# First transfers in another order, and two weight passes pinned on VectorE, in a windowed attention and three-way maxout kernel

## The chip, the cores and the metric

The kernel runs on one core of one Trainium2 chip. The metric is the device time of one execution in microseconds (us). All values are float32, or float32r, the same 32 bits read by TensorE as a matmul operand.

## What is computed

The reference, cut to what matters:

```python
# q, k, v: (8, 8, 576, 64): batch B, heads H, sequence S, head size D
scores = scale * np.matmul(q, k.transpose(0, 1, 3, 2))
bias = slopes[:, None, None] * (-np.abs(rel))[None, :, :]      # rel = i - j
mask = (rel >= 0) & (rel < 128)                                # a causal window of 128
scores = np.where(mask, scores + bias[None], -1e9)
attn = np.exp(scores - np.max(scores, axis=-1, keepdims=True))
attn = attn / (np.sum(attn, axis=-1, keepdims=True) + 1e-9)
o = np.matmul(attn, v)
x = o.transpose(0, 2, 1, 3).reshape(B * S, H * D)              # (4608, 512)
h = np.maximum(np.maximum(x @ w1, x @ w2), x @ w3)             # w1..w3: (512, 768)
return h @ w_out                                               # w_out: (768, 512)
```

## The kernel before, in words

**Attention.** The 64 heads are taken in pairs of a batch; a pair is a task (32 tasks, four to a batch). A task has rows in blocks of 128, the last block of 64 shared by two neighbouring tasks, so two tasks make nine steps and a batch of eight heads makes 18 (`steps`, `n_steps`). A step's work: `products` (the score matmuls into the PSUM tiles `ps_s` or `ps_m`, line 381, for two steps at once), `score` (on VectorE the copy under a mask, lines 396 and 399, then per head one pass that adds the bias, keeps the row maximum and writes the tile `s`, line 410), `exps` (two exponentials on ScalarE, line 422), `sums_of` (for two steps: ScalarE adds the epsilon to the sums, line 428, VectorE takes the reciprocal, line 429), `normalise` (GpSimd, line 436, or ScalarE, line 441), `turn` (four transposes on TensorE into `pt`, line 450, copied out by ScalarE and spread by GpSimd) and `mix` (the matmuls with v into `ps_x`, lines 495 and 517).

**Weights.** The 12 weight groups (`w_all`; 0 to 8 are w1 to w3 in slices, 9 to 11 are w_out) are each 1 MB. `fetch(g)` starts the transfer of a group into one of two raw buffers (tag `hs2`, shown as `hs`) on SyncE's queue, line 145. A group is copied as bytes without its first three, so that its words stand shifted; VectorE passes over the bytes and words then form the float32 values. `preparing()` takes the groups in the order 0, 1, 9, 10, 11, 2, ..., 8, each in six parts: `exponents` (for the first four groups, `few`, a clip of the exponent bytes on VectorE, line 156), `convert` (two VectorE passes of 1024 elements: the one that ends at line 165 is called the reduce here, the one at line 172 the shift), and four `part`s. Each part splits 512 columns into a high half on ScalarE (line 196) and a low half on VectorE (line 197), and for parts 2 and 3 TensorE first forms sums of weight blocks (the fold, line 201; line 187 for a low half that is formed there), which need the matrices `plus` (the identity) and `minus`. The results are the tiles `ring` (groups 0 to 8, two groups at a time) and `ow` (9 to 11). Groups 0 to 8 are also stored to HBM (`keep`, line 192) and come back from there for the later batches.

**Maxout.** With the seven-product scheme for 2x2 blocks, each batch has 77 units (`unit`, line 709) of up to 12 matmuls on `xs` (the attention output in high and low halves, `factors_x`) or `hs` (the hidden values, `factors_h`), and their results are combined on ScalarE and VectorE (lines 725, 662, 663).

**Order.** All calls are put in a list of events with a time in steps (`at(when, what, ...)`), sorted, and traced in that order. The scheduler behind the tracing then sets each engine's list by its own estimates of readiness; `tc.keep_in_program_order(x)` holds an instruction behind everything traced before it on its engine. `weights(n)` advances the preparation by n parts' worth: it is called at each step s + 0.2 from step 5 on with 1.6, which makes one or two parts. `spin` puts matmuls without use on TensorE. What stands ahead of the events is traced by hand, at the end of the function: the first transfers, the biases (`slopes`, `slopes_t`, from the tile `dist`), and `plus` and `minus` from `dist[:, 2]`, where the identity is loaded.

Of the kernel before, what the change touches and what calls it, by code (L numbers as in the profile page):

```python
# [15 lines left out]
ALU = mybir.AluOpType  # L16
# [18 lines left out]
def attention_maxout_kernel(  # L35
# [11 lines left out]
    nc = tc.nc  # L47
# [40 lines left out]
    for a in range(2):  # L88
        for d in (slice(0, P),) if a == 0 else (slice(0, D), slice(D, P)):
            nc.gpsimd.affine_select(  # L90
                out=prev[d, a], in_=prev[d, a], pattern=[[1, P]], compare_op=ALU.is_gt, fill=0.0,
# [7 lines left out]
    dist = hs_p.tile([P, 3, P], F32, name="hs")  # L99
# [5 lines left out]
    def slopes_t(pair):  # L105
        for h in range(2):
            d = slice(h * D, (h + 1) * D)
            for j in range(2):
                nc.gpsimd.tensor_scalar(
                    out=bias_t[d, pair, j], in0=dist[d, 1], scalar1=slope(4 * pair + 2 * h + j), scalar2=None,  # L110
                    op0=ALU.mult,
                )

    def slopes(hp):
        for h in (2 * hp, 2 * hp + 1):
            nc.scalar.activation(bias[:, h, :], dist[:, 0], AF.Copy, scale=slope(h))
        nc.gpsimd.affine_select(  # L117
            out=bias0[:, 2 * hp:2 * hp + 2], in_=bias[:, 2 * hp:2 * hp + 2], pattern=[[0, 2], [-1, P]],
            compare_op=ALU.is_ge, fill=-NEG, base=0, channel_multiplier=1,
        )  # L120
# [22 lines left out]
    def fetch(g):  # L143
        r = raws[g] = hs_p.tile([P, 4 * DM + DM // 2], I32, name="hs2", bufs=2)
        nc.sync.dma_start(r.bitcast(U8)[:, :16 * DM - 3], w_all[g].bitcast(U8)[:, 3:])

    def pieces(g):
        r = raws[g]
        x = r[:, :4 * DM].rearrange("p (n w) -> p n w", w=2)
        sign = r.bitcast(I8)[:, :16 * DM].rearrange("p (n b) -> p n b", b=8)[:, :, 4]  # L150
        return x[:, :, 0], x[:, :, 1], sign, r[:, 4 * DM:].bitcast(I8)

    def exponents(g, few):
        _, t, top, small = pieces(g)
        if few:
            nc.vector.tensor_scalar(out=small, in0=top, scalar1=-56.0, scalar2=56.0, op0=ALU.max, op1=ALU.min)
        else:
            nc.scalar.activation(small, top, AF.Relu, bias=-56.0)
            nc.scalar.activation(t.bitcast(F32), top, AF.Relu, scale=-2.0 ** 27, bias=-56.0 * 2.0 ** 27)
# [110 lines left out]
    def preparing():  # L270
        for n, g in enumerate(g_order):
            exponents(g, n < FEW)
            yield
            convert(g, n < FEW)
            yield
            for k in range(4):
                while g < 9 and not ahead(g, k > 0):
                    yield True
                part(g, k)
                if k == 1 and n + 2 < NG:  # L280
                    fetch(g_order[n + 2])
                yield
# [57 lines left out]
    def load(t):  # L340
        b, hp = tasks[t]
        qkt[t] = qk_p.tile([P, 2, S], F32, name="qk")
        for cs in (slice(0, 2 * P), slice(2 * P, S)) if t == 0 else (slice(0, S),):
            nc.sync.dma_start(qkt[t][:, :, cs], qk[b, hp, :, :, cs])

    def load_v(t):
        b, hp = tasks[t]
        vt[t] = v_p.tile([P, NB + 1, P], F32, name="v")
        nc.sync.dma_start(vt[t], v[b, hp])
# [384 lines left out]
    def at(when, what, *args):  # L734
        events.append((when, len(events), what, args))
# [40 lines left out]
            when += pace if u < 77 * b + 63 else O_PACE  # L776
    for u in range(77 * B, 77 * B + 3):
        at(when, unit, u)
    for s in range(5, n_steps + 2):
        at(s + 0.2, weights, 1.6)  # L780
        at(s + 0.7, rest)
    for s in range(1, n_steps, 2):
        at(s + 0.45, spin, SPIN)
# [5 lines left out]
    at(2 * n_steps + LAG_X + shift[2], fix)  # L789
    spin(FIRST_SPIN)  # L790
    load(0)
    load_v(0)
    nc.sync.dma_start(dist[:, 2], c_ident)
    slopes(0)
    slopes_t(0)
    fetch(0)
    nc.scalar.copy(out=plus, in_=dist[:, 2])
    nc.scalar.activation(minus, dist[:, 2], AF.Copy, scale=-1.0)
    load(1)
    fetch(1)  # L800
    for _, _, what, args in sorted(events, key=lambda e: e[:2]):
        what(*args)
# [38 lines left out]
```

## Time and profile before

| | |
|---|---|
| three timed runs | 773.58 us median (770.88, 773.58, 775.7) |
| the profiled execution | 771.28 us, of it 769.5 us span |
| TensorE busy (matmul) | 750.6 us |
| TensorE weight loads | 680.9 us |
| VectorE | 546.0 us |
| ScalarE | 519.0 us |
| GpSimd | 193.5 us |
| transfers | 184.95 MB, mean 240 GB/s |

The span runs from the first instruction to the last; the device time is 1.8 us longer. In rows of the profile PE is TensorE, PEld its weight loads, DVE VectorE, ACT ScalarE, POOL GpSimd and SP SyncE, whose queue starts most transfers. A row of the timeline gives the start, the duration, the engine, the line of the kernel, the operation, what it writes and reads, how many are merged, and in brackets how long the engine had been idle and what ended it.

### The profile page before, as it was taken

Reading aid. Unit: us, or ns where it says so; the run is one execution under the profiler, and the core shown is the slowest. Engines: PE = TensorE matmul, PEld = TensorE weight load, DVE = VectorE, ACT = ScalarE, POOL = GpSimd, SP = SyncE. Lnnn points to the kernel's source line nnn. Section 1 sums busy time; section 2 is a strip of 40 time slices with the busy share of each in tenths; the row PEclk is TensorE's granted clock in tenths of the full one; section 3 lists DMA queues with packets and bytes.
Section 4 is the critical chain, followed back from the end, with each engine's and each line's share of the span. In section 5 each row is a group of like instructions: output and inputs, shape, how many; then the busy total and the mean of one; then the engine's idle time right before and its main releaser. Section 6 shows DMA issues by size and latency. Waiting matters only on the chain.

```text
span 769.5 us, 19396 instructions
## 1 busy us (share of the span) xinstructions
PE 750.6 (98%) x7252; PEld 680.9 (88%) x7257; DVE 546.0 (71%) x1698; ACT 519.0 (67%) x1680; POOL 193.5 (25%) x403
## 2 busy tenths in 40 slices
PE   7898999999999999999999999999999999999998
PEld 3466778889999999999999999999999999999998
DVE  4869788885767847795677847695777847693673
ACT  5798798876678766776676756676676766552342
POOL 4440222311232122221222122221222122343100
PEclk9999999999999999999999999999999999999999
DMA  6772777584898559983888569883898568789721
GB/s 246 246 288 94 271 258 290 219 291 124 282 306 278 191 187 314 306 279 102 293 297 284 182 197 317 292 274 117 284 302 275 185 205 287 263 264 359 232 71 63
DMA packets 43838, 184.95 MB, mean 240 GB/s; under 512 B 4832, under 2 KB 14304, under 8 KB 34912
## 3 DMA queue, kind: packets, MB, share of 16 engines
q0 software_dynamic: 20304, 115.61, 45.5%
q1 hardware_dynamic: 23296, 67.97, 25.2%
q8 instruction: 57, 0.93, 0.5%
q14 instruction: 37, 0.30, 0.1%
q10 hardware_dynamic: 144, 0.13, 0.1%
HBM read 157.74 MB, written 25.95 MB: 239 GB/s over the span
## 4 chain that ended last, share of the span: by engine, by line
PE 67%; DVE 13%; ACT 7%; issue 1%; DVEq 0%; ACTq 0%
PE ps_m L709 54%; PE ps_s L381 4%; PE ps_x L517 4%; PE pt L450 3%; DVE hs L565 3%; DVE t L662 2%; DVE hq L663 2%; ACT p L422 2%; DVE t L568 1%; DVE xs L565 1%; PE pt L201 1%; ACT p L441 1%; ACT t L725 1%; DVE xk L551 1%; ACT hs L564 1%
## 5 line engine op out<-in xcount | busy, mean ns | idle before, releaser
L709 PE MATMUL ps_m<-xs,ring 128*128 128x288 f32 x2916 | 415.7, 297 | 3.1 <-ACT t L725 1.8
L709 PEld LDWEIGHTS ps_m<-xs,ring 128*128 128x128 f32 x2916 | 393.4, 188 | 10.3 <-ACT t L725 6.4
L725 ACT COPY t<-ps_m 128x288 f32<-128x288 f32 x262 | 102.5, 393 | 78.4 <-PE ps_m L709 76.0
L709 PE MATMUL ps_m<-hs,ow 128*128 128x288 f32 x1008 | 141.6, 297 | 1.1 <-DVE hs L565 0.4
L709 PEld LDWEIGHTS ps_m<-hs,ow 128*128 128x128 f32 x1008 | 134.8, 188 | 4.5 <-ACT t L725 1.9
L422 ACT ACTIVATE p<-s,st 128x128 f32<-128x128 f32 x288 | 115.0, 402 | 13.0 <-DVE st L410 12.0
L470 POOL TENSOR_SCALAR_AFFINE_SELECT pp<-pr 128x256 f32<-128x256 f32 x112 | 51.2, 457 | 287.9 <-ACT pr L454 167.2
L317 POOL DMA_DIRECT2D ring<-keep x121 | 65.0, 538 | 203.4 <-PE ps_m L709 196.5
L441 ACT ACTIVATE p<-p,st 128x128 f32<-128x128 f32 x252 | 85.8, 395 | 26.8 <-DVE st L429 26.8
L662 DVE TENSOR_TENSOR t<-ps_m,t 128x288 f32<-128x288 f32 x144 | 64.9, 452 | 50.3 <-PE ps_m L709 34.9
L410 DVE CUSTOM_DVE_ANT_0 s<-ps_s,bias 128x128 f32<-128x128 f32 x240 | 60.8, 285 | 10.5 <-POOL bias L117 4.5
L663 DVE TENSOR_TENSOR hq<-t,hq 128x288 f32<-128x288 f32 x144 | 65.7, 462 | 2.5
L381 PE MATMUL ps_s<-qk 64*64 64x192 f32 (+1 forms) x1088 | 63.3, 317 | 0.8 <-DMA qk<-in_qk 0.4
L517 PE MATMUL ps_x<-pp,v 64*64 64x64 f32 (+3 forms) x1456 | 56.2, 274 | 0.0
L422 ACT ACTIVATION_READ_ACCUMULATOR p<-s,st 128x1 f32 x288 | 55.6, 193 | 0.0
L564 ACT CAST hs<-hq 128x288 fp32r<-128x288 f32 x96 | 40.1, 433 | 22.7 <-DVE hq L663 19.3
L551 DVE TENSOR_TENSOR xk<-ps_x,xk 128x256 f32<-128x256 f32 (+3 forms) x56 | 25.4, 453 | 39.0 <-ACT xk L550 39.0
L517 PEld LDWEIGHTS ps_x<-pp,v 64*64 64x64 f32 x1456 | 42.8, 133 | 11.1 <-issue 9.8
L474 POOL TENSOR_SCALAR_AFFINE_SELECT pp<-pr 128x256 f32<-128x256 f32 (+1 forms) x112 | 50.1, 447 | 1.1
L450 PE MATMUL pt<-plus,p 128*128 128x128 f32 x288 | 48.3, 287 | 1.7 <-POOL p L436 1.0
L450 PEld LDWEIGHTS pt<-plus,p 128*128 128x128 f32 x288 | 30.3, 140 | 20.5 <-issue 14.0
L399 DVE COPY_PREDICATED ps_s<-prev,ps_s 128x256 f32<-128x256 uint8 x105 | 44.3, 422 | 3.7 <-PE ps_s L381 2.3
(123 smaller groups left out, 823.8 us busy)
## 6 DMA issues: line engine op xcount, KB each, us to landing
ring<-keep POOLq DMA_DIRECT2D x60, 1024.0 KB, 7.5
ring<-keep POOLq DMA_DIRECT2D x61, 768.0 KB, 5.9
qk<-in_qk SPq DMA_DIRECT2D x31, 576.0 KB, 5.6
hs<-in_w_all SPq DMA_DIRECT2D x12, 1023.6 KB, 5.6
v<-in_v SPq DMA_DIRECT2D x32, 320.0 KB, 5.6
keep<-ring SPq DMA_DIRECT2D x9, 1024.0 KB, 5.3
outT<-t SPq DMA_DIRECT2D x64, 144.0 KB, 1.8
keep<-ring SPq DMA_DIRECT2D x9, 768.0 KB, 4.9
```

The costliest lines, as they stand in the source:

```text
L317: nc.gpsimd.dma_start(wts[n, a], keep[n % 9][a])
L381: pe(nc.tensor.matmul(ps[j][d:d + D, o:o + k1 - k0], lhsT=qkt[u][j * D:(j + 1) * D, 0, q0:q0 + D], rhs=qkt[u][j * D:(j + 1) * D, 1, k0:k1] ...
L410: nc.vector.tensor_tensor_reduce(out=x, in0=ps[j][:, P:2 * P], in1=below, scale=-0.125, scalar=3.0e38, op0=ALU.add, op1=ALU.min, accum_out ...
L422: nc.scalar.activation(p[:, j], x, AF.Exp, bias=st[:, 0, a, j:j + 1], scale=-1.0, accum_out=st[:, 1, a, j:j + 1])
L441: nc.scalar.activation(p[:, j], p[:, j], AF.Copy, scale=st[:, 2, a, j:j + 1])
L450: pe(nc.tensor.transpose(out=pt[:, a, j], in_=p[:, j], identity=ident))
L470: nc.gpsimd.affine_select(out=old, in_=src, pattern=[[-x, n] for x, n in pat], compare_op=ALU.is_gt, fill=0.0, base=0, channel_multiplier=1,)
L517: pe(nc.tensor.matmul(x[j * D:(j + 1) * D, r, o:o + rhs.shape[1]], lhsT=vv[k, i, j * D:(j + 1) * D], rhs=rhs[k], start=start, stop=True, s ...
L662: nc.vector.tensor_tensor(out=s, in0=ps, in1=e, op=ALU.add)
L663: nc.vector.tensor_tensor(out=h, in0=s, in1=h, op=ALU.max)
L709: pe(nc.tensor.matmul(part_of[n, {2: 0, 5: 0, 6: 0, 3: 1}.get(kk, kk)], lhsT=lt, rhs=rt, start=first, stop=i == len(pairs) - 1, skip_group ...
L725: nc.scalar.copy(out=e, in_=ps)
```

## The change

The calls at the end of the function come in another order. SyncE's first transfers were: q and k of task 0 (in two pieces), v of task 0, the identity, weight group 0, q and k of task 1, weight group 1. Now they are: q and k of task 0, weight group 0, q and k of task 1, v of task 0, weight group 1; and the identity is loaded from ScalarE's queue. The clip of the exponent bytes is held in program order on VectorE for groups 0 and 1, and the first call of `weights` is now an event of its own, at 2.06, with one part; the call at step 5.2 has 0.6 in place of 1.6.

```diff
     def exponents(g, few):
         _, t, top, small = pieces(g)
         if few:
-            nc.vector.tensor_scalar(out=small, in0=top, scalar1=-56.0, scalar2=56.0, op0=ALU.max, op1=ALU.min)
+            x = nc.vector.tensor_scalar(out=small, in0=top, scalar1=-56.0, scalar2=56.0, op0=ALU.max, op1=ALU.min)
+            if g < 2:
+                tc.keep_in_program_order(x)
...
+    at(2.06, weights, 1)
     for s in range(5, n_steps + 2):
-        at(s + 0.2, weights, 1.6)
+        at(s + 0.2, weights, 1.6 if s > 5 else 0.6)
         at(s + 0.7, rest)
...
     load(0)
-    load_v(0)
-    nc.sync.dma_start(dist[:, 2], c_ident)
+    nc.scalar.dma_start(dist[:, 2], c_ident)
+    fetch(0)
     slopes(0)
     slopes_t(0)
-    fetch(0)
+    load(1)
+    load_v(0)
     nc.scalar.copy(out=plus, in_=dist[:, 2])
     nc.scalar.activation(minus, dist[:, 2], AF.Copy, scale=-1.0)
-    load(1)
     fetch(1)
```

With it, lines from 157 to 778 of the kernel move down by two, and those behind by three or more (410 becomes 412, 197 becomes 199, 793 becomes 795).

SyncE's list from its first transfer on, before (`qk`: q and k, `hs_164` and `hs_170`: the raw weights of groups 0 and 1):

```order
L344 DMA qk<-in_qk 128x2x256
L344 DMA qk<-in_qk 128x2x320
L349 DMA v<-in_v 128x640
L793 DMA hs<-in_ident 128x128
L145 DMA hs_164<-in_w_all 128x8189
L344 DMA qk<-in_qk 128x1152
L145 DMA hs_170<-in_w_all 128x8189
```

and of the change:

```order
L346 DMA qk<-in_qk 128x2x256
L346 DMA qk<-in_qk 128x2x320
L145 DMA hs_153<-in_w_all 128x8189
L346 DMA qk<-in_qk 128x1152
L351 DMA v<-in_v 128x640
L145 DMA hs_170<-in_w_all 128x8189
```

The identity has left this list, and v stands three transfers later. In ScalarE's list the identity's transfer stands second, and the casts to `plus` and `minus` stand behind two of the eight biases instead of all eight.

VectorE's list behind the low half of group 0's first fold (`hs_170`: group 1; `ps_m_453` and `ps_m_454`: the scores of steps 10 and 11), before:

```order
L197 TENSOR_TENSOR ring<-ps_m_401,ring 128x2x256
L410 ISA s,st<-ps_s,bias_115 128x128
L410 ISA st 128x1
L165 ISA hs_170<-hs_170 128x1024
L172 SCALAR_TENSOR_TENSOR hs_170<-hs_170 128x1024
L396 COPY_PREDICATED ps_m_453<-prev,ps_m_453 128x128
L429 RECIPROCAL st<-st 128x4
L396 COPY_PREDICATED ps_m_454<-prev,ps_m_454 128x128
```

and of the change, in which the clip (L156) of group 1 stood eight rows ahead before:

```order
L199 TENSOR_TENSOR ring<-ps_m_401,ring 128x2x256
L431 RECIPROCAL st<-st 128x4
L156 TENSOR_SCALAR hs_170<-hs_170 128x1024
L398 COPY_PREDICATED ps_m_453<-prev,ps_m_453 128x128
L398 COPY_PREDICATED ps_m_454<-prev,ps_m_454 128x128
L412 ISA s,st<-ps_m_453,bias 128x128
L412 ISA st 128x1
L412 ISA s,st<-ps_m_454,bias 128x128
L412 ISA st 128x1
L167 ISA hs_170<-hs_170 128x1024
L398 COPY_PREDICATED ps_m_453<-prev,ps_m_453 128x128
L174 SCALAR_TENSOR_TENSOR hs_170<-hs_170 128x1024
```

The reciprocal (of steps 8 and 9) has come ahead of group 1's three passes, and the passes now stand among the masks and scores of steps 10 and 11. Group 0's clip has moved back by one score.

TensorE's list where the fold of group 1 (`ps_m_507`) begins (`ps_m_610` and `ps_m_611`: the scores of steps 14 and 15), before:

```order
L201 MATMUL ps_m_507<-ring,plus 128x256 x2
L495 MATMUL ps_x<-pp,v 64x256 x4
L381 MATMUL ps_s<-qk 64x192
L381 MATMUL ps_m_610<-qk 64x128 x2
L381 MATMUL ps_m_611<-qk 64x128 x2
L381 MATMUL ps_m_610<-qk 64x256 x2
L381 MATMUL ps_m_611<-qk 64x256 x2
L201 MATMUL ps_m_507<-ring,plus 128x256 x4
```

and of the change:

```order
L497 MATMUL ps_x<-pp,v 64x256 x4
L383 MATMUL ps_s<-qk 64x192 x3
L383 MATMUL ps_m_610<-qk 64x128 x2
L383 MATMUL ps_m_610<-qk 64x256
L383 MATMUL ps_m_611<-qk 64x128
L203 MATMUL ps_m_507<-ring,plus 128x256 x2
L383 MATMUL ps_m_611<-qk 64x128
L383 MATMUL ps_m_610<-qk 64x256
L383 MATMUL ps_m_611<-qk 64x256
L203 MATMUL ps_m_507<-ring,plus 128x256 x4
```

The fold's first two matmuls have moved back behind five score matmuls and four of `mix`.

## The prediction

> **What bounds the kernel now.** I read the summary lines first, then the ten-microsecond windows, then the start row by row. A window's row gives its stretch and length, the busy time of TensorE, its weight loads, VectorE, ScalarE and GpSimd, the granted TensorE clock, and the transfers' share and GB/s.
>
> ```profile
> span 769.5 us, 19396 instructions
> PE 750.6 (98%) x7252; PEld 680.9 (88%) x7257; DVE 546.0 (71%) x1698; ACT 519.0 (67%) x1680; POOL 193.5 (25%) x403
> ...
> 30.00:40.00 10.00, 7.86 (x69) 4.82 (x70) 8.94 (x30) 7.68 (x26) 4.03 (x7) 1.00 0.79 278
> ...
> 60.00:70.00 10.00, 8.65 (x62) 6.80 (x61) 9.36 (x16) 9.68 (x21) 0.00 (x0) 1.00 0.17 42
> ```
>
> Over the whole span TensorE is the bound: 750.6 of 769.5 us, so 18.9 us idle. The orders of the two kernels differ on every engine but GpSimd, and there only in about the first 70 to 90 us; behind that each engine runs the same list. In that stretch no engine is full at first: from 30 to 40 us TensorE has 7.86 of 10, VectorE 8.94, ScalarE 7.68. From 60 to 70 us ScalarE (9.68) and VectorE (9.36) nearly are. So the start is a mesh of short waits ahead of a stretch without slack, and what the change is worth is the time by which the list that both kernels share starts earlier or later. That is small beside 771.28 us, the profiled execution's own time (1.78 us of it outside the span).
>
> **The transfers.** Columns of the first kind of row: start, duration, engine, line, what is written and read, and in brackets the idle time before and what ended it; of the second: size and us from issue to landing.
>
> ```profile
> 2.16 0.59 SPq L349 DMA_DIRECT2D v<-in_v  x1
> 3.27 0.43 SPq L145 DMA_DIRECT2D hs<-in_w_all  x1
> 3.74 0.44 SPq L344 DMA_DIRECT2D qk<-in_qk  x1
> ...
> v<-in_v SPq DMA_DIRECT2D x1, 320.0 KB, 4.0
> hs<-in_w_all SPq DMA_DIRECT2D x1, 1023.6 KB, 6.3
> qk<-in_qk SPq DMA_DIRECT2D x1, 576.0 KB, 7.3
> ...
> 6.35 0.30 ACT L797 CAST plus<-hs 128x128 fp32r<-128x128 f32 x1 [1.70 <-DMA hs<-in_ident]
> 6.92 0.29 DVE L410 CUSTOM_DVE_ANT_0 s<-ps_s,bias 128x128 f32<-128x128 f32 x1 [4.53 <-POOL bias L117]
> 10.18 0.69 DVE L156 TENSOR_SCALAR hs<-hs 128x1024 int8<-128x1024 int8 x1
> 11.04 0.77 PE L381 MATMUL ps_s<-qk 64*64 64x192 f32 x14 [0.41 <-DMA qk<-in_qk]
> 12.19 0.55 PE L450 MATMUL pt<-plus,p 128*128 128x128 f32 x3 [0.38 <-POOL p L436]
> 17.65 0.65 PE L495 MATMUL ps_x<-pp,v 128*64 128x256 f32 x2
> ```
>
> Before, v lands at 2.16 + 4.0 = 6.2 us, weight group 0 at 3.27 + 6.3 = 9.6, the second q and k at 3.74 + 7.3 = 11.04, the moment at which TensorE goes on. Between the last two landings 576 KB arrive in 1.47 us, 390 KB a us. Without v's 320 KB ahead of them both land 0.8 us sooner, at 8.8 and 10.2; v lands at about 11.0, and the second weight group where it did.
> - *q and k:* the 0.41 us wait at 11.04 goes. But the transpose behind it waits until 12.19 for GpSimd's product, which does not come from this transfer, so TensorE only idles later: taken at 0, the row at 12.19 being the next on its engine; the ends are -0.41 and 0.
> - *Group 0's weights* had landed 0.6 us before their first pass at 10.18, which did not wait: 0. In an execution whose transfer is later by more than 0.6 us that pass stalls VectorE, and the 0.8 us would cover it: a gain of some tenths that this profile cannot show.
> - *Identity on ScalarE's queue:* ScalarE's 1.70 us wait for it goes, but what comes behind, the first exponential, needs the first score at 6.92: 0. Its issue (nearest row: 0.43 us on SP's queue) stands ahead of the biases. The score at 6.92 needs the first masked bias, which is ready some 3 us sooner: 0; without that cover it would be 0.43.
> - *v* is read at 17.65, over 6 us behind its new landing: 0.
>
> **The first pass, pinned.** It changes places with one score, 0.69 us against 0.29; the same work still lies ahead of the next mask, so 0.
>
> **The second group's passes** are where the order really changes. VectorE, ScalarE and TensorE before:
>
> ```profile
> 22.58 0.77 DVE L156 TENSOR_SCALAR hs<-hs 128x1024 int8<-128x1024 int8 x1
> 25.66 0.69 DVE L197 TENSOR_TENSOR ring<-ps_m,ring 128x512 fp32r<-128x512 f32 x1 [1.47 <-ACT ring L196]
> 26.48 1.22 DVE L165 CUSTOM_DVE_ANT_0 hs<-hs 128x1024 int32<-128x1024 int8 x1
> 27.73 1.25 DVE L172 SCALAR_TENSOR_TENSOR hs<-hs 128x1024 uint32<-128x1024 uint32 x1
> 29.33 0.30 DVE L396 COPY_PREDICATED ps_m<-prev,ps_m 128x128 f32<-128x128 uint8 x1 [0.35 <-PE ps_m L381]
> 30.33 0.30 DVE L396 COPY_PREDICATED ps_m<-prev,ps_m 128x128 f32<-128x128 uint8 x1 [0.63 <-PE ps_m L381]
> 33.92 0.43 DVE L399 COPY_PREDICATED ps_s<-prev,ps_s 128x256 f32<-128x256 uint8 x1 [0.66 <-PE ps_s L381]
> 35.39 0.68 DVE L197 TENSOR_TENSOR ring<-hs,ring 128x512 fp32r<-128x512 f32 x1
> 39.30 0.28 DVE L410 CUSTOM_DVE_ANT_0 s<-ps_s,bias_t 128x128 f32<-128x128 f32 x1
> 40.84 0.29 DVE L410 CUSTOM_DVE_ANT_0 s<-ps_m,bias 128x128 f32<-128x128 f32 x1 [0.41 <-ACT p L422]
> 42.15 0.29 DVE L410 CUSTOM_DVE_ANT_0 s<-ps_m,bias 128x128 f32<-128x128 f32 x1 [0.68 <-ACT p L422]
> 48.07 0.43 DVE L399 COPY_PREDICATED ps_s<-prev,ps_s 128x256 f32<-128x256 uint8 x1 [1.27 <-PE ps_s L381]
> ...
> 25.04 0.59 ACT L196 CAST ring<-ps_m 128x512 fp32r<-128x512 f32 x1 [0.98 <-PE ps_m L201]
> 28.66 0.21 ACT L428 ACTIVATE st<-st 128x4 f32<-128x4 f32 x1
> 36.62 0.40 ACT L441 ACTIVATE p<-p,st 128x128 f32<-128x128 f32 x1 [1.59 <-DVE st L429]
> ...
> 36.13 0.74 PE L201 MATMUL ps_m<-ring,plus 128*128 128x256 f32 x4 [1.60 <-DVE ring L197]
> 38.04 0.66 PE L450 MATMUL pt<-plus,p 128*128 128x128 f32 x4
> ```
>
> Now the reciprocal of steps 8 and 9 stands ahead of the clip, and the pin holds the clip behind it. It needs ScalarE's sum, at 28.66 before and about 28.35 now, since an exponential from behind the copy at 25.04 moves into the 0.98 us ahead of it. VectorE, free at about 26.3 (25.66 + 0.69), waits some 2.2 us with the group's three passes (0.77 + 1.22 + 1.25 = 3.24 us) queued behind; before, two of them filled just this gap. I followed the new order by hand with the old durations and waits. The clip runs from 28.65 to 29.3, the scores of step 10 to 31.0, the reduce to 32.15, the shift from 32.35 to 33.5, the scores of step 11 to 34.2, the two low halves of the ring to 35.5 (before, the second ended at 35.39 + 0.68 = 36.07), step 12's mask from 35.5 (before 33.92), step 13's first score from 40.5 (before 39.30). So by 40 us VectorE is 1.2 us late with scores: some 2.8 us more idle before 29, less the waits of 0.35, 0.63 and 0.66 that it now does without.
>
> TensorE and ScalarE gain at the same place. Before, the second group's fold, the matmuls at 36.13, held TensorE for 1.60 us, and with it the transposes of steps 8 and 9 at 38.04. With the ring's halves there at 35.5 the fold starts 0.6 us sooner; one score group that now stands between takes some of it back, and the transposes come at about 37.6. ScalarE's wait until 36.62 ends at about 36.0, since that reciprocal now stands ahead of the next group's clip. VectorE's lag then meets waits of 0.41, 0.68 and 1.27 us at 40.84, 42.15 and 48.07, together 2.36, that were for ScalarE and TensorE, which are not late: it is gone by 48 us, ahead of the full stretch at 60. I take TensorE's lead at 38.04, -0.4 us, as what is left: it is the row on the engine that bounds the rest. The ends are -1.6, the whole wait at 36.13 won and kept, and +1.2, the whole lag kept.
>
> **The sum** is 0 + 0 + 0 - 0.4 = -0.4 us, so 770.9 for an execution like the profiled one.
>
> **Rivals.** *A: the cold window goes.* The first rows give stretch, length, TensorE busy, granted clock and transfers.
>
> ```profile
> 6.47:9.88 3.41, 3.24 (x32) 1.00 1.00 405
> 9.88:13.30 3.42, 2.41 (x22) 1.00 0.82 314
> 13.30:16.71 3.41, 3.19 (x16) 0.50 0.58 213
> ...
> 17.27 0.30 DVE L396 COPY_PREDICATED ps_m<-prev,ps_m 128x128 f32<-128x128 uint8 x1 [2.07 <-PE ps_m L381]
> 18.59 0.59 ACT L454 COPY pr<-pt 128x512 f32<-128x512 f32 x1 [1.99 <-PE pt L450]
> ```
>
> Behind a stretch in which TensorE is busy 2.41 of 3.42 us its clock is halved for 3.41 us, which withholds 1.7. VectorE and ScalarE wait 2.07 and 1.99 us for the matmuls in it, so all of the 1.7 is on the path. If the earlier q and k keep TensorE busy enough, the time is 771.28 - 0.4 - 1.7 = 769.2. For it: 0.41 us of the idle time between 9.88 and 13.30 is this transfer's. Against it: that time only moves to just before 12.19, inside the same stretch. The Trainium skill, page "TensorE: Matmul & The Clock Gate", Part 1, says that the clock drops after an idle window of about 3.4 us, and that the windows run free of a kernel's start. The trace agrees on the length but not on idleness, with 2.41 us busy. By the rule of free windows the cold one comes and goes by chance in both kernels, and the time would be the forecast's.
>
> *B: TensorE's whole wait at 36.13 is won,* and the shared list starts 1.6 us sooner: 769.7. For it: the wait is on the bounding engine. Against it: in the new order the halves are ready only 0.6 us sooner.
>
> *C, slower: VectorE's lag is kept.* The place is the reciprocal near 28.5 with 3.24 us of passes behind it; the price is 1.2 us, and 2.8 where none of the waits behind 29 gives way; it decides from the point where ScalarE waits for scores near 41 us rather than VectorE for ScalarE. Time 772.5 to 774.1. For it: VectorE is the busiest engine from 30 to 40, 8.94 of 10. Against it: its waits at 40.84 and 42.15.
>
> *D: the change doesn't do what it says.* Group 0 had landed before its pass, so the pin protects from nothing, and the rest moves idle time alone: 771.3.
>
> **How the numbers follow.** The four times of before are 770.88, 771.28, 773.58 and 775.7, mean 772.9; the profiled one is low among them, and the median 2.3 above it. Less 0.4, and less a few tenths for executions in which group 0 lands late, I forecast 772.0 for a median. Chances: the forecast 0.40, D 0.15, A 0.12, B 0.13, C 0.16, and 0.04 for what no row shows. The range goes from the lowest time less B's 1.6 and half of A's 1.7, 768.4, rounded to 768.0, up to the highest with most of C's 1.2, 776.5. All the cases lie within 1% (7.7 us), about what a measurement of this kernel can tell from no change; beyond it I leave 0.05 for faster and 0.03 for slower, A and B together outweighing C.
>
> **What would show it.** Right: no wait for q and k near 11 us, VectorE idle some 2 us ahead of a reciprocal near 28.5, a shorter wait for the ring near 36, and TensorE's rows from 100 us on shifted by under 1 us. Wrong: a shift of over 2 us by 60 us, a half-clock window gone or added, or new waits of VectorE for ScalarE beyond 50 us.

## The result, and the profile after

The changed kernel takes **777.89 us** (median of 22 runs, 774.25 to 783.02) against 773.2 us for the kernel before in the same runs: a ratio of 1.0066, with a 95% interval of 1.0052 to 1.0079. It is slower by 4.7 us where 772.0, and no more than 776.5, was forecast. Its profiled execution took 779.36 us.

The summary of that execution, and its ten-microsecond windows (stretch and length, busy time of TensorE, weight loads, VectorE, ScalarE and GpSimd, granted clock, transfers' share and GB/s):

```profile
span 777.7 us, 19405 instructions
PE 754.1 (97%) x7257; PEld 682.0 (88%) x7257; DVE 546.1 (70%) x1698; ACT 518.7 (67%) x1680; POOL 196.2 (25%) x403
...
30.00:40.00 10.00, 7.94 (x60) 4.11 (x54) 8.19 (x26) 6.15 (x19) 4.02 (x5) 0.83 0.60 224
40.00:50.00 10.00, 8.10 (x60) 4.64 (x59) 6.98 (x21) 7.15 (x24) 3.10 (x5) 1.00 0.77 254
50.00:60.00 10.00, 9.32 (x67) 6.09 (x67) 6.06 (x19) 7.57 (x26) 6.40 (x10) 1.00 0.70 254
60.00:70.00 10.00, 9.28 (x72) 5.49 (x72) 7.20 (x16) 8.80 (x20) 3.20 (x6) 1.00 0.44 144
```

The work of VectorE and ScalarE is the same to 0.3 us. TensorE is busy 3.5 us longer, of which 1.7 are a slower clock, as shown below, and idle 23.6 us instead of 18.9. Two windows of before, not shown with the prediction, say why idleness here is dear:

```profile
40.00:50.00 10.00, 9.77 (x74) 6.00 (x73) 7.57 (x24) 9.00 (x28) 4.81 (x7) 1.00 0.84 320
50.00:60.00 10.00, 9.85 (x76) 5.97 (x76) 5.81 (x19) 9.01 (x24) 5.25 (x11) 1.00 0.56 211
```

TensorE has 9.77 and 9.85 of 10 there, ScalarE 9.00 and 9.01: for these two engines the stretch without slack begins at 40 us, not at 60 as the prediction had it. In the changed kernel ScalarE has 7.15 and 7.57 in the same two windows, 3.3 us less.

**The place.** One row that both kernels have is a clock for the shift: four transposes at 30 us, and four at the end of the first batch's weights. Before:

```profile
30.23 0.66 PE L450 MATMUL pt<-plus,p 128*128 128x128 f32 x4
...
85.88 0.63 PE L450 MATMUL pt<-plus,p 128*128 128x128 f32 x4 [0.56 <-ACT ring L188]
```

TensorE of the changed kernel, with the folds and the mix between:

```profile
30.24 0.66 PE L452 MATMUL pt<-plus,p 128*128 128x128 f32 x4
...
32.70 0.65 PE L497 MATMUL ps_x<-pp,v 128*64 128x256 f32 x4 [1.01 <-POOL pp L472]
34.40 0.91 PE L497 MATMUL ps_x<-pp,v 128*64 128x256 f32 x4 [1.05 <-POOL pp L472]
...
36.73 0.80 PE L203 MATMUL ps_m<-ring,plus 128*128 128x256 f32 x2
...
40.68 0.66 PE L452 MATMUL pt<-plus,p 128*128 128x128 f32 x4
...
93.28 0.63 PE L452 MATMUL pt<-plus,p 128*128 128x128 f32 x4 [0.58 <-ACT ring L190]
```

Up to 30.24 nothing is lost. From there to the end of the weights it takes 63.04 us instead of 55.65: **7.4 of the 8.2 us** by which the spans differ. The transposes forecast for 37.6 come at 40.68, behind two waits of 1.0 us for GpSimd's masked tiles that before did not have. The stretch with those waits, and the next of the same length at half clock:

```profile
31.25:34.66 3.41, 1.35 (x12) 0.48 (x9) 3.32 (x9) 2.54 (x9) 3.07 (x4) 1.00 0.77 320
34.66:38.07 3.41, 3.41 (x26) 1.73 (x22) 3.03 (x10) 2.02 (x8) 0.95 (x2) 0.50 0.24 55
```

TensorE is busy 1.35 of 3.41 us and then runs 3.41 us at half clock: 1.7 us of the 7.4. VectorE in this stretch did what was followed by hand:

```profile
29.30 0.18 DVE L431 RECIPROCAL st<-st 128x4 f32<-128x4 f32 x1 [2.25 <-ACT st L430]
...
34.45 1.40 DVE L199 TENSOR_TENSOR ring<-hs,ring 128x512 fp32r<-128x512 f32 x2
```

It idles 2.25 us (2.2 forecast), and the ring's halves end at 35.85 (35.5 forecast). The transfers, as size and us from issue to landing, and TensorE's wait for the second q and k:

```profile
qk<-in_qk SPq DMA_DIRECT2D x1, 576.0 KB, 9.3
v<-in_v SPq DMA_DIRECT2D x1, 320.0 KB, 9.7
...
12.16 0.77 PE L383 MATMUL ps_s<-qk 64*64 64x192 f32 x14 [1.14 <-DMA qk<-in_qk]
```

The second q and k, issued nearly 1 us sooner, behind the 1 MB weight group, land at 12.1, 1.1 us later than before, where 0.8 sooner was forecast. The windows from 5 to 10 us show the rate at which the queues fill, before:

```profile
5.00:10.00 5.00, 4.71 (x42) 1.86 (x40) 1.74 (x12) 1.51 (x7) 4.47 (x10) 1.00 1.04 406
```

and after:

```profile
5.00:10.00 5.00, 5.00 (x42) 1.94 (x40) 1.35 (x8) 1.95 (x10) 4.57 (x10) 1.00 0.91 332
```

332 GB/s arrive instead of 406, some 0.4 MB less in the 5 us. Why the same queue is slower in this order, no run here shows.

### The profile page after: what moved, and what is told of

It reads as the page before. It is cut to its first block, busy times and chain, and to the rows that moved or that the text cites. A ratio compares the mean times of both kernels' runs of the same rounds, so it can differ in the third digit from the quotient of the medians.

```text
span 777.7 us, 19405 instructions
## 1 busy us (share of the span) xinstructions
PE 754.1 (97%) x7257; PEld 682.0 (88%) x7257; DVE 546.1 (70%) x1698; ACT 518.7 (67%) x1680; POOL 196.2 (25%) x403
## 4 chain that ended last, share of the span: by engine, by line
PE 65%; DVE 12%; ACT 7%; issue 1%; DMA 1%; DVEq 0%; ACTq 0%
PE ps_m L711 53%; PE ps_s L383 4%; PE ps_x L519 4%; PE pt L452 3%; DVE hs L567 2%; ACT p L424 2%; DVE t L664 2%; DVE hq L665 2%; DVE t L570 1%; DMA ring<-keep 1%; ACT t L727 1%; DVE xs L567 1%; PE pt L203 1%; ACT p L443 1%; ACT hs L566 1%
## 5 line engine op out<-in xcount | busy, mean ns | idle before, releaser
L383 PEld LDWEIGHTS ps_s<-qk 64*64 64x64 f32 x1088 | 40.3, 135 | 8.7 <-issue 4.4
```

The costliest lines, as they stand in the source:

```text
L383: pe(nc.tensor.matmul(ps[j][d:d + D, o:o + k1 - k0], lhsT=qkt[u][j * D:(j + 1) * D, 0, q0:q0 + D], rhs=qkt[u][j * D:(j + 1) * D, 1, k0:k1] ...
```

## The experiments

The theories, as they stood in turn. **T**: the transfers cost it. **P**: the pin of group 1's clip costs it, and then how: **H**, GpSimd's selects are held up by VectorE passes that read two SBUF inputs; **L**, VectorE's passes are late and the lag is kept; **C**, the half-clock window behind the idle time; **S**, the scheduler, which takes VectorE to be late behind the pin, rewrote the lists of all engines from about 36 to 62 us, and that order costs it. The expectations call P theory O and C theory K. All times are medians; each ratio is to the kernel before in the same runs, with its 95% interval.

**Transfers or pins.** Only the transfers (the pin of group 1 taken away, which gives back the lists of before):

```diff
-            if g < 2:
+            if g < 1:
```

> The change with the pin on group 0 alone: its transfers stay reordered, TensorE's, GpSimd's and SyncE's later lists are those of before, VectorE's differs by the one swapped pair at group 0's clip. Theory O (the place of group 1's passes on VectorE costs the time): within 1 us of before, 772 to 774 median, no wait of TensorE for GpSimd's selects near 32 and 34 us, no half-clock window near 35 us. Theory T (the reordered transfers cost it: group 0 and the second q and k landed 1.1 us later in the profile of the change): 776 to 778, and the lag is there by 13 us and stays.

Only the pins (the kernel before, with this and nothing else of the change):

```diff
+            if g < 2:
+                tc.keep_in_program_order(x)
...
+    at(2.06, weights, 1)
...
-        at(s + 0.2, weights, 1.6)
+        at(s + 0.2, weights, 1.6 if s > 5 else 0.6)
```

> The transfers of before with the pins and the early weight event: every engine's list behind the first transfers is that of the change. Theory O: as the change, 776 to 779 median, spread to 783, with the waits for GpSimd near 32 and 34 us and the 3 us wait of VectorE for group 10's weights near 43 us. Theory T: as before, 772 to 774.

And the change once more:

> The change itself, on the same chip as the other three: 776 to 779 median, between 774 and 783. By all theories the runs with a mean granted clock near 1.0 lie near 774.5, and those with less are longer by about the clock time withheld, (1 - clock) times the span.

The transfers alone: 772.14 us, ratio 1.0 (0.9986 to 1.0014). The pins alone: 779.73, 1.0094 (1.0066 to 1.0123). The change: 778.5, 1.0073 (1.005 to 1.0096). TensorE with the transfers alone:

```profile
11.99 0.77 PE L383 MATMUL ps_s<-qk 64*64 64x192 f32 x14 [1.16 <-DMA qk<-in_qk]
...
86.37 0.63 PE L452 MATMUL pt<-plus,p 128*128 128x128 f32 x4 [0.56 <-ACT ring L190]
```

The late landing is here too, but the shift row comes at 86.37, 0.5 us later than before instead of 7.4. T falls; the pin of one instruction, with what follows from it, costs all that these runs can tell. (The pins alone came out 0.7 us above the 776 to 779 expected of them.)

**A wait that looks like the price.** VectorE of the changed kernel waits 3.02 us at 45.75 for the weights of group 10. Pinning that group's clip too moves it:

```diff
-            if g < 2:
+            if g in (0, 1, 10):
```

> The change with group 10's clip pinned too, so that it stands behind the scores of steps 14 to 17 on VectorE instead of ahead of the second score of step 14. Theory O with three parts (GpSimd held by the passes, half clock, VectorE waiting 3.02 us for group 10's transfer): the 3.02 us wait goes and 1 to 3 us with it, 775 to 777, still over before. If that wait was hidden: as the change, 777 to 778.

The wait for the transfer is gone, the time is not better: 778.9, ratio 1.0081 (1.0058 to 1.0103). But at 46.60 VectorE now waits 2.46 us for ScalarE's cast of `ow`, so one wait has only taken the place of another. The run shows that nothing is won by sparing VectorE this transfer; whether VectorE's waits here are on the path it doesn't show.

**Is GpSimd held?** In the changed kernel VectorE's reduce and shift come to stand beside the selects of the mix. First, the change with the passes held behind those scores and the later calls of `weights` put off:

```diff
+            if g == 1:
+                tc.keep_in_program_order(x)
...
-        at(s + 0.2, weights, 1.6 if s > 5 else 0.6)
+        at(s + 0.2, weights, 0.6 if s == 5 else -0.4 if s == 10 else 1.6)
...
+    at(11.1, weights, 2)
```

> The changed kernel, with the reduce and the shift of weight group 1 moved further back on VectorE, behind the scores of step 11; its clip stays where the change has it. GpSimd's and SyncE's lists are the change's, VectorE's differ in about 24 rows of 1700. Theory H (GpSimd is held): in the change the first two selects behind 31.5 us take 1.05 and 1.38 us in place of 0.41 because the reduce (31.15) and the shift (32.49) run beside them, and TensorE's mixes wait 1.01 and 1.05 us for them. Without the two passes beside them the selects take about 0.41 us each, both waits go, and the time falls by their 2 us at least, with the half-clock window behind them by up to 3.7: 774.8 to 776.5 against 778.5 of the change. Theory L (VectorE is merely late): the passes and the ring halves behind them come some 1.5 us later still, so the time is that of the change or up to 2 us above: 778.5 to 780.5.

It took 780.46, ratio 1.0105 (1.0085 to 1.0125): what L expects, not what H does. TensorE there:

```profile
34.85 0.65 PE L499 MATMUL ps_x<-pp,v 128*64 128x256 f32 x4 [1.05 <-POOL pp L474]
...
39.78 1.83 PE L205 MATMUL ps_m<-ring,plus 128*128 128x256 f32 x6 [3.15 <-DVE ring L201]
```

The passes now make TensorE wait 3.15 us for the ring, so this run puts another loss in the place of the first. Nor are the selects free in it: the reduce runs at 33.25, and the select beside it, at 33.41, takes 1.39 us, which is TensorE's wait of 1.05. So it alone does not clear the selects. So the selects by themselves: the kernel before with six stretches behind its end, each with four selects on GpSimd, five of them beside three instructions of one kind on VectorE (the time of the kernel has no meaning here).

```diff
+        for _ in range(3):
+            x = kind()
...
+        for _ in range(4):
+            tc.keep_in_program_order(nc.gpsimd.affine_select(
+                out=dst, in_=src, pattern=[[0, 2], [1, P]], compare_op=ALU.is_ge, fill=0.0, base=0, channel_multiplier=-1,
```

> The kernel before, with six short stretches behind its end, some 15 us in all: in each, GpSimd makes four selects of 128x256 f32 and VectorE runs three instructions of one kind beside them, on data of its own: none; the shift; the reduce; the clip; a subtraction with both inputs in SBUF (128x512 f32); the same with one input in PSUM. The time is therefore not to be compared. Theory H: a select takes about 0.41 us with nothing beside it and beside the subtraction from PSUM, 1.0 to 1.45 beside the shift and the reduce, 0.7 to 0.9 beside the subtraction within SBUF. For the clip, one select of 0.86 us in the kernel before began while a clip ran, so 0.41 or 0.86 are both open. Theory L: about 0.41 in every stretch.

GpSimd's rows: alone, beside three shifts, three clips, three subtractions with both inputs in SBUF, and three that read one input from PSUM:

```profile
771.20 1.83 POOL L838 TENSOR_SCALAR_AFFINE_SELECT t<-t 128x256 f32<-128x256 f32 x4 [29.21 <-DVE t L832]
773.49 4.43 POOL L838 TENSOR_SCALAR_AFFINE_SELECT t<-t 128x256 f32<-128x256 f32 x4 [0.46 <-DVE t L832]
...
783.28 2.83 POOL L838 TENSOR_SCALAR_AFFINE_SELECT t<-t 128x256 f32<-128x256 f32 x4 [0.46 <-DVE t L832]
...
786.57 2.83 POOL L838 TENSOR_SCALAR_AFFINE_SELECT t<-t 128x256 f32<-128x256 f32 x4 [0.46 <-DVE t L832]
...
789.87 1.84 POOL L838 TENSOR_SCALAR_AFFINE_SELECT t<-t 128x256 f32<-128x256 f32 x4 [0.46 <-DVE t L832]
```

Four selects take 1.83 us alone, 4.43 beside the shifts (and as much beside the reduces), 2.83 beside the clips, 2.83 beside subtractions within SBUF and 1.84 beside those that read PSUM. Where they are held, they take 0.6 us more than the three VectorE instructions (3.84 for the shifts, 2.25 for the clips, 2.24 for the subtractions), as if each waited for one of them to end. That agrees with the Trainium skill, page "SBUF — State Buffer", section "Who interferes with whom": VectorE and GpSimd share a port pair as an exclusive lock, a VectorE instruction with two SBUF inputs contends with a GpSimd one that reads SBUF, and one with at most one SBUF input does not, unless it runs in a mode that uses both ports. Whether the clip, which has one input and holds all the same, runs in such a mode no run here shows. The holds are real. Are they paid for? The kernel before with two more VectorE instructions ahead of step 11's masks, of one length, once a kind that holds and once a kind that doesn't (the result of neither is used):

```diff
+            tc.keep_in_program_order(nc.vector.tensor_tensor_reduce(
+                out=small, in0=top, in1=small, scale=1.0, scalar=0.0, op0=ALU.subtract, op1=ALU.max, accum_out=None,
...
+    at(10.21, beside, 2)
```

> The kernel before, its weight passes where they are, with two more instructions on VectorE near 31.6 us, one ahead of each of the two masks of step 11, just where the change has the reduce and the shift: each is the reduce once more (two inputs in SBUF, about 1.22 us), and its output is read by nothing. All five lists are equal to those of g2 but for these two. Theory H: the selects of 31.6 us take 1.0 to 1.4 us in place of 0.41, TensorE waits about 1 us for each of the first two, and the time goes up by 2 to 4 us on that of g2. Theory L: g1 and g2 are within 0.7 us of each other.

```diff
+            tc.keep_in_program_order(nc.vector.tensor_reduce(
+                out=small[:, :1], in_=top, op=ALU.max, axis=mybir.AxisListType.X
...
+    at(10.21, beside, 2)
```

> As g1, but each of the two instructions is a maximum over the 1024 strided bytes, with one input in SBUF and about as long (1.1 to 1.2 us), so VectorE is as late as in g1. Theory H: the selects take about 0.41 us, TensorE's waits for them stay under 0.4 us each, and the time is within 1.2 us of the kernel before: 772 to 773.3. Theory L (a late VectorE alone does it): both are some 3 to 4 us slower than the kernel before, 775 to 776.

With two inputs, GpSimd and TensorE:

```profile
32.23 1.47 POOL L477 TENSOR_SCALAR_AFFINE_SELECT pp<-pr 128x256 f32<-128x256 f32 x1 [6.16 <-ACT pr L461]
...
33.75 0.65 PE L502 MATMUL ps_x<-pp,v 128*64 128x256 f32 x4 [0.84 <-POOL pp L477]
```

With one input:

```profile
31.23 0.41 POOL L477 TENSOR_SCALAR_AFFINE_SELECT pp<-pr 128x256 f32<-128x256 f32 x1 [6.16 <-ACT pr L461]
...
31.84 1.22 PE L502 MATMUL ps_x<-pp,v 128*64 128x256 f32 x8
```

The select takes 1.47 us in the one and 0.41 in the other, TensorE waits for it in the one alone, and the times can't be told apart: 778.47, ratio 1.0084 (1.0055 to 1.0112), and 778.25, 1.008 (1.0057 to 1.0103). H falls as the main cause: the hold is there, and the 2 to 4 us that it was to cost are not, though with six runs of each, spread over 5 to 6 us, a smaller price could hide. Besides, some 2.4 us of harmless work on VectorE cost as much as the change, and 2 us more than L had expected. So it need not be the pinned passes as such, and what the scheduler makes of a busier VectorE comes into question.

**The clock window.** Matmuls without use in TensorE's waits, in the changed kernel and in the kernel before (the latter twice):

```diff
+    at(10.0035, spin, 5)
```

> The changed kernel with five more of the idle matmuls (0.39 us each, 1.95 in all) put on TensorE's list just ahead of the mixes near 32.7 us, where it waits 1.01 and 1.05 us; the other engines' lists are the change's. Theory K (clock): the half-clock window of 34.66 to 38.07 follows from TensorE being busy too little just before; with the waits filled it goes, the mean clock is 0.997 or more, and the time falls by about the 1.7 us that one such window withholds: 776 to 777.3 against 778.5. If the windows are only incidental, the time stays at 778.5 within 0.7. In either case the part of the loss that is waiting for GpSimd (theory H) stays, so not under 775.

```diff
+    at(3.2, spin, 2)
```

> The kernel before with two more idle matmuls on TensorE ahead of the second pair's q and k, where it waits 0.39 us near 9.7 and 0.41 near 10.6; no other list differs. Theory K: TensorE is then busy 3.2 of the 3.42 us ahead of the half-clock window at 13.30, which goes, and with it up to 1.7 us: 770.9 to 771.8 against 772.5. If the window's cause is another, the time stays at 772.5, or goes up by the few tenths by which the two push the matmuls behind them.

> The kernel before with the two idle matmuls ahead of the second pair's q and k, once more, for a narrower interval of the version that may beat both. If the half-clock window near 13.3 us costs its 1.2 us in most executions, the median is 770 to 771.5 and the ratio 0.998 to 0.999; if that one measurement was chance, 772 and a ratio of 1.000.

The change with spins took 778.37, ratio 1.0082 (1.0065 to 1.0099): 1.1 us above the range of C, and within the one expected if the windows are only incidental. Its windows:

```profile
31.15:34.56 3.41, 2.21 (x16) 0.88 (x13) 3.32 (x9) 2.53 (x9) 3.08 (x4) 1.00 0.74 308
34.56:37.97 3.41, 3.41 (x35) 2.09 (x32) 3.41 (x10) 2.00 (x8) 0.94 (x2) 1.00 0.41 120
```

With 2.21 busy in place of 1.35 the clock stays full in this execution. But over its runs the clock withholds 3.1 us on the mean (3.3 in the change), and the median is no better: the clock withholds as much elsewhere, so this run neither shows nor refutes C. What speaks against C as the whole is the last column of the table below. Before with spins took 770.62, 0.9989 (0.9973 to 1.0005), and in the repetition 773.48, 1.0008 (0.9991 to 1.0024), above both values that were expected of it. Whether spins help the kernel before stays open; no version was found that beats it.

**Late passes or rewritten lists.** Four kernels in which every engine's list is written out by hand, by holding each instruction behind the one that is to stand ahead of it (`ORDER` gives the place of each):

```diff
+    for engine, text in ORDER.items():
+        moved = [int(x.split("x")[0]) for x in text.split() for _ in range(int((x + "x1").split("x")[1]))]
+        row = [lists[engine][k + m] for k, m in enumerate(moved)]
+        for one, two in zip(row, row[1:]):
+            tc.add_manual_dep(
+                two, one.name,
```

The first has the lists of the change up to the second ring half of group 1, near 36 us, and behind it the order of before: the passes are late, the rest isn't rewritten.

> The transfers of the kernel before. The lists of VectorE, ScalarE and TensorE are the change's up to the second low half of ring for weight group 1 (the passes stand behind the reciprocal, as in the change), and behind that the order of the kernel before; they differ from it in 24, 12 and 14 rows. Theory L (the lateness costs): 775 to 779, as with the whole change. Theory S (the lists behind it cost): 771.5 to 774.

The second is its mirror image: before up to there, the order of the change behind.

> The reverse: transfers and lists of the kernel before up to the same low half, with group 1's passes at their early place, and behind that the order of the change; 42, 46 and 108 rows of VectorE, ScalarE and TensorE differ from the kernel before. Theory S: 775.5 to 779. Theory L: 771.5 to 774.

The third has the lists of before and in them only the two single-input VectorE instructions of above; the fourth the lists that the scheduler had made for those two instructions, without the two.

> The lists of the kernel before, with the two instructions of g2 (a maximum over 1024 bytes, 1.2 us each, GpSimd not held) ahead of the two masks of step 11; nothing else is moved. VectorE is 2.4 us late from there. Theory L: 775.5 to 778.5, as g2's 778.25. Theory S: 772 to 774.5, since VectorE has waits behind 40 us that take the 2.4 up.

> The lists of g2 without its two instructions: VectorE is not late, but stands in the order that the scheduler wrote for a late one; 50 rows of VectorE, 36 of ScalarE and 186 of TensorE differ from the kernel before. Theory S: 775.5 to 778.5. Theory L: 771.5 to 774.

The table has the time withheld by the clock (one less the mean granted clock, times the span, mean over the runs; the clock has three decimals, so 0.4 us either way in one run) and the median of the time less that, "at full clock".

| | median | ratio (95%) | withheld | at full clock |
|---|---|---|---|---|
| before, beside the four | 772.52 | | 1.9 | 770.5 |
| the change, 22 runs | 777.89 | 1.0066 (1.0052–1.0079) | 3.3 | 774.4 |
| late passes, later order of before | 775.56 | 1.0037 (1.0021–1.0052) | 4.3 | 771.3 |
| lists of before, then the change's | 778.33 | 1.007 (1.0046–1.0094) | 3.1 | 775.1 |
| lists of before, two more on VectorE | 774.74 | 1.0033 (1.0012–1.0053) | 4.2 | 770.9 |
| the rewritten lists without the two | 774.93 | 1.0033 (1.0018–1.0049) | 1.4 | 773.9 |

**The rewritten lists alone cost 5.8 us, as much as the change**, and 4.6 of them at full clock. Lateness alone costs 3.0 and 2.2 us, of it 0.8 and 0.4 at full clock, which is within the scatter of the runs: the rest is half-clock windows behind the idle time that it gives TensorE. So S holds for the change, with some of L and C besides; the two halves do not add (3.0 + 5.8 against 5.4 to 5.9 for the change and 7.2 for the pins alone). The fourth kernel bears S out on another rewritten list, but in part: that list is 2.4 of the 5.4 us that the two instructions had cost (3.4 us at full clock), and the third kernel has their lateness at 2.2.

By what was expected, only the second kernel hits S's range. The first lies in L's, the third 0.2 us above S's, the fourth between the two ranges: neither theory holds alone. Lists held in the order of before, with nothing else, were not run; the third kernel, which holds them and has two instructions more, is 0.4 us above before at full clock, so the holding itself can cost little. With late passes, the transposes by which the shift is read, and the clock's windows:

```profile
31.22 0.66 PE L458 MATMUL pt<-plus,p 128*128 128x128 f32 x4
...
90.80 0.63 PE L458 MATMUL pt<-plus,p 128*128 128x128 f32 x4 [0.56 <-ACT ring L196]
...
35.00:40.00 5.00, 4.62 (x30) 2.69 (x31) 4.92 (x15) 2.36 (x8) 1.13 (x3) 0.62 0.45 151
40.00:45.00 5.00, 4.33 (x23) 2.69 (x22) 2.95 (x10) 3.02 (x10) 1.76 (x3) 0.69 0.79 326
```

59.58 us between them, 3.9 more than before, of which the clock withholds 5 x 0.38 + 5 x 0.31 = 3.5. With the rewritten lists alone, TensorE, VectorE and ScalarE:

```profile
30.05 0.66 PE L458 MATMUL pt<-plus,p 128*128 128x128 f32 x4
...
40.06 0.65 PE L503 MATMUL ps_x<-pp,v 128*64 128x256 f32 x2 [1.53 <-POOL pp L478]
40.63 0.50 PE L209 MATMUL ps_m<-ring,minus 128*128 128x256 f32 x2
...
43.88 0.66 PE L458 MATMUL pt<-plus,p 128*128 128x128 f32 x4
...
89.94 0.63 PE L458 MATMUL pt<-plus,p 128*128 128x128 f32 x4 [0.56 <-ACT ring L196]
...
37.58 0.69 DVE L205 TENSOR_TENSOR ring<-ps_m,ring 128x512 fp32r<-128x512 f32 x1 [1.20 <-ACT ring L204]
...
38.52 1.22 DVE L180 SCALAR_TENSOR_TENSOR hs<-hs 128x1024 uint32<-128x1024 uint32 x1
...
41.64 0.59 ACT L230 CAST ring<-ps_m 128x512 fp32r<-128x512 f32 x1 [1.90 <-PE ps_m L209]
42.13 0.65 ACT L204 CAST ow<-hs 128x512 fp32r<-128x512 f32 x1
```

and the same instructions before:

```profile
38.51 0.50 PE L201 MATMUL ps_m<-ring,minus 128*128 128x256 f32 x2
...
39.81 0.86 PE L495 MATMUL ps_x<-pp,v 128*64 128x256 f32 x6 [0.32 <-POOL pp L470]
...
42.65 0.66 PE L450 MATMUL pt<-plus,p 128*128 128x128 f32 x4
...
36.50 1.20 DVE L172 SCALAR_TENSOR_TENSOR hs<-hs 128x1024 uint32<-128x1024 uint32 x1
37.76 0.69 DVE L197 TENSOR_TENSOR ring<-ps_m,ring 128x512 fp32r<-128x512 f32 x1
...
37.93 0.67 ACT L196 CAST ow<-hs 128x512 fp32r<-128x512 f32 x1
```

Here 59.89 us lie between, 4.2 more than before. TensorE's rows show the first piece. Before, the rest of the fold (38.51) runs as soon as VectorE's low half ends (37.76 + 0.69), and the mix behind it waits 0.32 us for GpSimd's masked tile. In the rewritten list the mix stands ahead of the fold: TensorE waits 1.53 us for that tile, and the fold, whose low half ended at 38.27, comes at 40.63. That is 1.2 us more of waiting, and the transposes that stood at 42.65 come at 43.88. In the changed kernel the mix, at 42.44, stands ahead of the fold too, at 43.01, and TensorE waits 1.10 us for it.

The other engines show the same. VectorE ran group 9's shift (36.50) while ScalarE made the ring's high half; now the low half comes first and waits 1.20 us for ScalarE, and the shift, queued behind it, ends at 39.74 in place of 37.70. ScalarE's cast of `ow`, which needs the shift, has come to stand behind a cast (41.64) that waits 1.90 us for the late fold, and runs at 42.13 in place of 37.93. Work that filled a wait before stands behind the wait now, and from 40 us on TensorE and ScalarE have 9 of 10 to do.

The second piece comes later. Between 60 us and the last transposes of the stretch (89.94, and 93.28 in the change) the waits that TensorE's rows show are 0.72, 0.93, 0.49, 0.41 and 1.33 with the rewritten lists alone and 0.72, 0.93, 0.49, 0.41 and 1.40 in the change; before, up to 85.88, they are 0.56, 0.63, 0.16 and 0.55. That is 3.9 and 4.0 us against 1.9. With the first 1.2 us it makes 3.2 of the 4.2. None of these waits was taken away singly.

## Why the prediction was wrong, point by point

- **Transfers, identity, first pass: 0 each.** Right as prices: the transfers alone give a ratio of 1.0. The landing was wrong by 1.9 us, 1.1 later in place of 0.8 sooner: the working took the rate at which the queue fills as given, and it fell, from 406 to 332 GB/s. That the 0 held in spite of it is luck in part: in the profile of that run the shift row is 0.5 us late, too little for its times to tell. The first score was misread, too: by the row at 6.92 it follows the bias that GpSimd masks just before, not one that is ready 3 us sooner, and it came at 7.07, 0.15 us late.
- **VectorE up to 36 us.** Right: 2.25 us of stall against 2.2, the low halves' end at 35.85 against 35.5.
- **The step that failed: "it is gone by 48 us".** The waits of 0.41, 0.68 and 1.27 that were to swallow VectorE's lag were read from before's list, as if the list behind 36 us were the same. It is another one, and the sum has no term for its order. That term is the greater part of the loss: 5.8 us by itself, 4.6 of it at full clock, begun where the mix stands ahead of a fold that could run. The text itself says that the orders differ up to 70 to 90 us; it priced only the first piece of the difference.
- **Nor does the lag vanish.** With the lists of before it is kept in part, 0.4 to 0.8 us at full clock. The gain on TensorE, -0.4 at 38.04, did not come: the transposes came 2.6 us late.
- **Rival A had the sign of the clock wrong.** The window at 13.30 did not go; a second one came at 34.66, behind a stretch in which TensorE, by its two waits for GpSimd, is idle 2.06 of 3.41 us. Only its removal was priced, never a new one.
- **Rival C**, slower by 1.2 to 2.8 us, had the right sign and stall. Its case in pure form, lateness alone, measured 2.2 to 3.0, mostly by clock and not by waits, so its figure came out for another reason than the one given; the change went beyond it by the rewritten lists.
- **B and D** fall: the fold of group 1, at 36.13 before, comes at 36.73, not at 34.5; and D can't hold where the pins alone add 7.2 us (779.73 against 772.55).

## What to carry to other kernels

A pin, or an instruction moved, changes what the scheduler thinks of an engine's time, and so every list behind it: compare the lists to their end, and look in each for ready work that now stands behind a wait. Follow the new list, not the old one's waits, and price it against the windows in which engines are full. To tell an instruction's own price from that of the rewritten order, freeze the lists and put the one without the other.

## What the runs showed of the hardware

- **GpSimd's selects are held beside VectorE passes, at no price that these runs can tell.** A select takes 1.47 us in place of 0.41 beside a pass with two SBUF inputs; the kernels' medians are 778.47 and 778.25 us.
- **How little busy time halves the clock is not settled.** Windows of about 3.41 us with 1.35 us busy (the change) and 2.41 of 3.42 (before) were followed by half clock, one with 2.21 (with spins) was not. The Trainium skill, page "TensorE: Matmul & The Clock Gate", Part 1, has the clock drop after an idle window of about 3.4 us: the length agrees, but busy time within the window, as the trace sums it, does not decide alone.
- **A transfer issued sooner can land later.** 576 KB of q and k took 9.3 us behind the 1 MB group; before, issued 0.9 us later and with v's 320 KB ahead of that group, 7.3.
